# A fused S4 convolution and gated unit on one core: another split of the kernel spectrum, table casts by transfers, additions by identity matmuls, and a new static order

## The chip, the cores and the metric

The kernel runs on one core of a Trainium2 chip. The metric is the device time of one execution in microseconds (us). TensorE (PE), VectorE (DVE), ScalarE (ACT), GpSimd (POOL) and SyncE (SP) each execute their own instructions in order; SP here only issues transfers, and POOL and ACT issue some too. Work on different engines is ordered by semaphores alone. Matmuls accumulate in PSUM, from where VectorE or ScalarE has to evict a result; the other tiles lie in SBUF.

## The reference

With L = 2048 tokens, D = 512 channels, N = 128 modes per channel and F = 1792 hidden columns, all arrays in bf16:

```python
xn  = layernorm(x)                                  # over the 512 channels
dt  = exp(log_dt);  A = A_re + 1j * A_im
P   = exp(dt * A * l)                               # 512 x 128 x 2048, l is a bf16 array
K   = sum over n of (C * P * dt * B), real part     # 512 x 2048: one filter for each channel
y   = irfft(rfft(xn padded) * rfft(K padded))[:2048] + xn * Dskip
glu = (sigmoid(xn @ w_gate) * (xn @ w_up)) @ w_down
out = x + y + glu
```

The lags l are held in bf16, so above 256 they are rounded to multiples of 2, 4 and 8: only some hundreds of different lags occur, and a filter can be put together from few powers.

## The kernel before, in words

**Order.** No scheduler decides on the chip. Every piece of work is an operation of a planner (`_Plan`, `pl.add`), with an engine, dependencies and buffers to take and give back; the list `ORDER` (above line 286) then holds all operation numbers in the order in which they are emitted, and each engine runs its own in that order. Three more lists choose engines: `ON_DVE` names the evictions and copies (`pl.copy`, L287 to L290) that VectorE does, the others being ScalarE's; `UEV` names the up projections that ScalarE evicts (L1066) before VectorE's product, which for the others reads PSUM; `ON_ACT` names the row tiles whose layer norm moments ScalarE takes. PSUM has two pairs of banks (128x1024 f32) and four single banks.

**Layer norm.** 16 row tiles of 128x512. VectorE takes moments (`bn_stats` L547, `bn_aggr` L548) of 15, ScalarE (L541, L542) of one. Per group of tiles `ln_small` takes the reciprocal root, partly by `pow` on POOL (L482, L483), and VectorE a reciprocal (L508); L555 (ScalarE) or L560 (VectorE) normalises. Transposed copies of xn feed the gated unit.

**Ladder.** From dt, exp and sin (L611 to L656) VectorE makes w = exp(dt A) in f32 and squares it again and again (ScalarE squares, L672; VectorE L679 and L681): 12 levels w, w^2, w^4 ... Each level is cast to bf16 (`f_cast`), by ScalarE (L666) or VectorE (L664), into the tables `W`. The f32 levels live in three rotating buffers.

**Tables and filter.** For each of four chunks of 128 channels, complex multiplications (`cmul`: L737 and L738 multiply by the real and the imaginary part of a level, L742 and L743 add) and squares (ScalarE L790, VectorE L795 and L796) build two tables for each channel: G, 16 powers times C·dt·B, and H, 41 powers. A 32-column matmul for each channel (L821) gives all 16x41 lags. The result is evicted (`kq`), put in another order by selection matmuls (L841) and evicted as `kT`, to which VectorE adds Dskip at one row (L852). G has two buffers, used in turn by the chunks.

**Convolution.** L698 transforms xn along blocks of tokens and writes the result to DRAM (`z_scr`). 16 units follow, eight for each half of the channels: load 256 KB of `z_scr`; L892, second step of the transform, four matmuls of 64x64; eviction to `xx`; a second copy of `xx` with its 32-row halves exchanged, in the first half by four transfers of 64 KB from SBUF to SBUF, in the second by four VectorE copies (L905); load 320 KB of constants (`c_E`); L914, ten full matmuls of 256 columns, which make the filter's spectrum of that unit from `kT`; eviction to `kb`; the products L919 (2048 elements) and L923 (1024) on VectorE; L936, the first step back, 16 matmuls of 64x64; eviction; write of 256 KB to DRAM (`v_scr`). When all units of a part are written, loads of `v_scr` in another order follow, and the last step back, L995. L997 adds a correction for a few last lags, made from `f_pre` on POOL (L712 to L716), L955 and L972.

**Gated unit.** Four groups of 512 tokens; each has 14 gate projections (L1031, sigmoid L1043), 14 up projections (L1055), products (L1070) and four down projections of 14 matmuls (L1099). For the first three groups the result is evicted to `glu_sb` and x is added by accumulating transfers that POOL issues (L1136); `final` then has VectorE add that and L995's result (L1010). The last group's down projections run into the PSUM bank that L995 adds to, and VectorE adds x (L1119).

Weights and rows are loaded in an order that is written out (`load`), the gate weights in three pieces.

Of the kernel before, what the change touches and what calls it, by code (L numbers as in the profile page):

```python
# [10 lines left out]
BF = mybir.dt.bfloat16  # L11
# [8 lines left out]
L = 2048  # L20
# [11 lines left out]
NGE = 16  # L32
NH = 41
NHP = 96
CUT_G = (0, 3 * 128, 7 * 128, 14 * 128)
CUT_U = (0, 7 * 128, 14 * 128)
NU = 16
NKT = 5
# [21 lines left out]
LAG0 = [0, 1, 3, 5, 7, 6, 4, 2, 8, 10, 14, 12, 9, 11, 13, 15, 256, 262, 260, 258, 264, 266, 270, 268, 524, 520, 516, 512, 780, 776, 772, 768,  # L60
        1024, 1032, 1544, 1536, 1280, 1288, 1800, 1792, 2048]
EXP = {5: 1, 9: 1, 10: 1, 11: 3, 17: 1, 21: 1, 22: 1, 23: 3, 24: 3, 25: 1, 26: 1, 28: 3, 29: 1, 30: 1, 33: 3, 34: 3, 35: 1, 37: 3, 38: 3, 39: 1}
# [31 lines left out]
def _build_M2():  # L94
# [3 lines left out]
    for g in range(NU):  # L98
        for par in range(2):
# [17 lines left out]
            M2[g, blk, blk] = M  # L117
    return M2

def _build_MAB():  # L120
# [4 lines left out]
    for g in range(NU):  # L125
        for par in range(2):
# [27 lines left out]
            MA[g, blk, blk] = A  # L154
            MB[g, blk, blk] = B
    return MA, MB

def _row(l):

    v = int(np.float32(ml_dtypes.bfloat16(l)))  # L160
    seg = range(0, 16) if v < 256 else range(16, 24) if v < 512 else range(24, 32) if v < 1024 else range(32, 40) if v < 2048 else (40,)
    for h in seg:
        if v >= LAG0[h] and (v - LAG0[h]) % 16 == 0 and (v - LAG0[h]) // 16 < NGE:
            return h, (v - LAG0[h]) // 16
    raise ValueError(l)

def _build_E(M2, by):

    E = np.zeros((NKT, 8, NGE, NU, 128))
    z = M2.reshape(NU, 2, 2, 32, 128)  # L170
    s1 = _build_S1(64).reshape(64, NU, 2, 2)
    for l in range(L):
        h, i = _row(l)
        if h < 40:
            m = (l - 1024 * (h >= 32)) % 2048
            E[h // 8, h % 8, i] += 2.0 ** EXP.get(h, 0) * np.einsum("gpc,gpcf->gf", s1[m // 32], z[:, :, :, m % 32, :])
    E = E.reshape(NKT, 128, NU, 128).transpose(1, 2, 0, 3)[:, by]
    E[:, 1::2] = np.roll(E[:, 1::2], 64, axis=-1)
    return E

def _consts():
    S1 = _build_S1()
    M2 = _build_M2()
    MA, MB = _build_MAB()
    by = np.arange(NU).reshape(2, NU // 2).T.reshape(NU)

    def quads(m, cross=False):
        m = m.transpose(1, 0, 2)
        lo, hi = m[0:64, :, 0:64].copy(), m[64:128, :, 64:128].copy()
        if cross:  # L190
            lo[:, 1::2], hi[:, 1::2] = m[64:128, 1::2, 64:128], m[0:64, 1::2, 0:64]
        return np.concatenate([lo, hi], axis=0)

    f = lambda v: np.ascontiguousarray(v.astype(np.float32)).astype(ml_dtypes.bfloat16)
    sw = np.zeros((128, 8, 48))
    for q in range(128):
        sw[q, 2 * (q // 32) + q % 2, 16 + q % 32 // 2] = 1.0
    sr = np.zeros((128, 4, 64))
    for q in range(8):
        sr[q, q // 2, 31 + 32 * ((q ^ (q // 2)) % 2)] = 1.0  # L200
    return dict(SR=f(sr), ident=f(np.eye(128)), S1=f(np.tile(S1, (4, 1))), S2=f(np.stack([_build_S2(by), np.roll(_build_S2(by), 32, axis=1)], axis=1)), M2=f(quads(M2[by])), SW=f(sw),
                MAB=f(np.stack([quads(MA[by], True), quads(MB[by], True)], axis=2)), E=f(_build_E(M2, by).reshape(128, NU // 2, 2, NKT, 128).transpose(1, 0, 2, 3, 4)))

UEV = (3, 5, 8, 9, 10, 11, 15, 16, 17, 18, 19, 20, 21, 23, 24, 26, 27, 28, 29, 30, 31, 32, 33, 34, 35, 36, 37, 38, 39, 40, 41, 42, 43, 44, 45, 54)
ON_DVE = (64, 67, 73, 76, 97, 98, 110, 121, 122, 123, 124, 482, 836, 838)
ON_ACT = (2,)
ORDER = [
# [987 lines left out]
```

## Time and profile before

| | |
|---|---|
| runs shown | 222.72, 221.31, 222.79 us; median 222.72 |
| profiled execution | span 219.8 us from the first to the last instruction; the page gives no other time of it |
| TensorE clock granted | 0.999 |
| transfers | 41.36 MB in 40651 packets |

The median of the runs is 2.9 us above the span. The page divides the span into 40 slices and gives the busy share of each in tenths (9 is 90% or more):

```profile
PE   7999988999999999999999999999989999999994
...
DVE  3999999999999999999999999999989999993582
ACT  3699999999999999769899999977578978942000
```

TensorE and VectorE are busy almost throughout; ScalarE has room in the second half and little to do in the last eighth. In the groups, a line gives engine, operation, shapes and count, then busy time and the mean of one in ns, and then the idle time of the engine just before:

```profile
L737 DVE TENSOR_TENSOR big<-big 128x2048 bf16<-128x2048 bf16 x4 | 4.9, 1231 | 0.0
L679 DVE SCALAR_TENSOR_TENSOR big<-big 128x512 f32<-128x512 f32 x11 | 7.6, 690 | 0.0
L672 ACT ACTIVATE big<-big 128x1024 f32<-128x1024 f32 x11 | 12.4, 1129 | 0.2 <-DVE big L664 0.2
```

An instruction's busy time overlaps that of the next by a little, so in the chain of waits (the work that ended last, followed back from the end) the same instruction counts a little less.

### The profile page before, as it was taken

How to read it: one execution, taken by the hardware profiler on the slowest of the kernel's cores; microseconds unless marked ns; L12 is line 12 of the kernel's file. 1: busy time of each engine (PE TensorE's matmuls, PEld its weight loads, DVE VectorE, ACT ScalarE, POOL GpSimd, SP SyncE). 2: the span in 40 equal slices, each digit the busy share in tenths (PEclk: the TensorE clock that was granted, in tenths of full speed). 3: DMA queues.
4: the chain of work that ended last, by engine and by line, in shares of the span. 5: the costliest groups of instructions: out<-in, count | busy, mean ns of one | idle time of the engine just before them, and what ended most of it. 6: DMA issues, size and time to landing. Idle time of an engine off the chain costs nothing.

```text
span 219.8 us, 5357 instructions
## 1 busy us (share of the span) xinstructions
PE 209.2 (95%) x2075; PEld 105.0 (48%) x2103; DVE 202.2 (92%) x444; ACT 175.9 (80%) x283; POOL 22.6 (10%) x39
## 2 busy tenths in 40 slices
PE   7999988999999999999999999999989999999994
PEld 2544433444434454445555555554555455543453
DVE  3999999999999999999999999999989999993582
ACT  3699999999999999769899999977578978942000
POOL 2216001001000049100000004000020100000000
PEclk9999999999999999999999999999999999999999
DMA  5997069216667064526818579856857987688743
GB/s 172 333 425 298 7 180 317 80 42 143 237 134 206 18 198 97 202 82 178 244 55 237 152 244 210 212 173 169 228 111 236 265 265 232 189 234 209 220 158 136
DMA packets 40651, 41.36 MB, mean 188 GB/s; under 512 B 9009, under 2 KB 31922, under 8 KB 40498
## 3 DMA queue, kind: packets, MB, share of 16 engines
q1 hardware_dynamic: 39458, 39.12, 57.7%
q0 software_dynamic: 864, 1.57, 4.9%
q10 hardware_dynamic: 304, 0.33, 0.6%
q8 instruction: 16, 0.26, 0.5%
q14 instruction: 9, 0.07, 0.1%
HBM read 25.28 MB, written 12.06 MB: 170 GB/s over the span
## 4 chain that ended last, share of the span: by engine, by line
DVE 48%; PE 41%; DMA 4%; ACT 4%; issue 2%; POOL 0%; DVEq 0%; ACTq 0%
PE bank L1099 11%; DVE big L738 7%; PE pair L914 7%; DVE big L737 6%; PE bank L1031 6%; PE bank L1055 6%; DVE hT_sb L1070 6%; PE pair L936 5%; DVE stats L547 4%; DVE big L742 4%; DVE big L743 3%; DVE big L679 3%; DVE big L681 3%; DMA big<-c_E 3%; ACT big L290 3%; DVE big L613 2%
## 5 line engine op out<-in xcount | busy, mean ns | idle before, releaser
L290 ACT ACTIVATE big<-pair 128x1024 bf16<-128x1024 f32 (+2 forms) x75 | 73.4, 996 | 9.2 <-PE pair L936 1.9
L1055 PE MATMUL bank<-xnT,wu_sb 128*128 128x512 bf16 x214 | 54.4, 379 | 2.5 <-ACT us_sb L1066 1.3
L1031 PE MATMUL bank<-xnT,wg_sb 128*128 128x512 bf16 (+1 forms) x211 | 50.9, 367 | 1.4 <-ACT xnT L576 0.4
L1099 PE MATMUL bank<-wd_sb,hT_sb 128*128 128x512 bf16 (+1 forms) x230 | 50.2, 366 | 0.4
L1043 ACT ACTIVATE hT_sb<-bank 128x512 bf16<-128x512 f32 x52 | 32.1, 643 | 3.8 <-PE bank L1031 3.6
L1031 PEld LDWEIGHTS <-wg_sb 128*128 128x128 bf16 x236 | 21.9, 98 | 26.4 <-issue 5.2
L1099 PEld LDWEIGHTS <-hT_sb 128*128 128x128 bf16 x238 | 22.5, 98 | 24.8 <-issue 2.1
L1055 PEld LDWEIGHTS <-wu_sb 128*128 128x128 bf16 x224 | 21.0, 97 | 27.2 <-issue 5.4
L737 DVE TENSOR_TENSOR big<-big 128x1024 bf16<-128x1024 bf16 (+4 forms) x40 | 26.8, 670 | 0.1
L738 DVE TENSOR_TENSOR big<-big 128x1024 bf16<-128x1024 bf16 (+4 forms) x40 | 26.6, 666 | 0.0
L1066 ACT ACTIVATE us_sb<-bank 128x512 bf16<-128x512 f32 x36 | 22.4, 634 | 0.0
L919 DVE TENSOR_TENSOR big<-big 128x2048 bf16<-128x2048 bf16 x16 | 19.5, 1219 | 0.4
L914 PE MATMUL pair<-big 128*128 128x256 bf16 x160 | 19.8, 272 | 0.1
L914 PEld LDWEIGHTS <-big 128*128 128x128 bf16 x160 | 15.5, 98 | 4.9 <-issue 1.1
L790 ACT ACTIVATE sq_sb<-big 128x256 bf16<-128x256 bf16 (+2 forms) x20 | 13.7, 685 | 3.9 <-DVE big L743 3.8
L743 DVE TENSOR_TENSOR big<-big 128x512 bf16<-128x512 bf16 (+4 forms) x40 | 16.6, 414 | 0.0
L742 DVE TENSOR_TENSOR big<-big 128x512 bf16<-128x512 bf16 (+4 forms) x40 | 16.5, 413 | 0.0
L290 ACT ACTIVATE big<-big 128x256 bf16<-128x256 bf16 x36 | 15.7, 470 | 0.2
L1070 DVE TENSOR_TENSOR hT_sb<-hT_sb,us_sb 128x512 bf16<-128x512 bf16 x36 | 14.9, 421 | 0.0
L905 DVE COPY big<-big 32x1024 bf16<-32x1024 bf16 x32 | 13.5, 421 | 0.5
L1070 DVE TENSOR_TENSOR hT_sb<-hT_sb,bank 128x512 bf16<-128x512 bf16 x20 | 13.2, 684 | 0.5 <-PE bank L1055 0.5
L936 PE MATMUL pair<-big 64*64 64x512 bf16 (+1 forms) x256 | 12.8, 326 | 0.5 <-ACT big L290 0.2
(103 smaller groups left out, 222.2 us busy)
## 6 DMA issues: line engine op xcount, KB each, us to landing
big<-c_E SPq DMA_DIRECT2D x16, 320.0 KB, 4.4
z_scr<-big SPq DMA_DIRECT2D x16, 256.0 KB, 3.0
big<-z_scr SPq DMA_DIRECT2D x16, 256.0 KB, 3.5
v_scr<-big SPq DMA_DIRECT2D x16, 256.0 KB, 2.9
big<-in_A_u_dram SPq DMA_DIRECT2D x4, 512.0 KB, 8.5
big<-big SPq DMA_DIRECT2D x32, 64.0 KB, 3.1
big<-v_scr SPq DMA_DIRECT2D x4, 512.0 KB, 5.0
wu_sb<-in_B_w_up_dram SPq DMA_DIRECT2D x2, 896.0 KB
```

The lines of the kernel that those rows point to most:

```text
L290: nc.scalar.activation(out=get(out), in_=get(in_), func=ACT.Identity)
L737: V.tensor_tensor(out=wide(outp), in0=wide(lo), in1=mre, op=ALU.mult)
L738: V.tensor_tensor(out=wide(tb()), in0=wide(lo), in1=mim, op=ALU.mult)
L742: V.tensor_tensor(out=outp[:, :, 0], in0=outp[:, :, 0], in1=tb()[:, :, 1], op=opr)
L743: V.tensor_tensor(out=outp[:, :, 1], in0=outp[:, :, 1], in1=tb()[:, :, 0], op=opi)
L914: T.matmul(two(sk)[:, o:o + DW], es()[:, g, kt, :], kT[p][:, kt, :], start=kt in (0, NKT - 1), stop=kt >= NKT - 2)
L936: T.matmul(two(sv)[o:o + 64, DW * (2 * g + y):2 * DW * (g + 1)], mab[b:b + 64, 2 * u + g, q, :], pq()[b:b + 64, q, ch] if y else pp()[b:b ...
L1031: T.matmul(bank(sl, k % 2)[:, c0:c1], w_at(w, CUT_G, kt, k), xnT[:, grp, kt, c0:c1], start=(kt == 0), stop=(kt == KT - 1))
L1043: S.activation(out=hT_sb[:, hs.idx, k % 2, :], in_=bank(sl), func=ACT.Sigmoid)
L1055: T.matmul(bank(sl), w_at(wu_sb, CUT_U, kt, k), xnT[:, grp, kt, :], start=(kt == 0), stop=(kt == KT - 1))
L1070: V.tensor_tensor(out=h(), in0=h(), in1=us_sb[:, us.idx, :] if on else bank(sl), op=ALU.mult)
L1099: T.matmul(bank(po)[:, 0:c[1] - c[0]], hT_sb[:, hts[k // 2].idx, k % 2, jj * 128:(jj + 1) * 128], wd_sb[:, k, c[0]:c[1]], start=first and ...
```

## The change

- **Tables.** G now has 32 entries for each channel, H 21. H is made for two chunks at once. G has one buffer instead of two. L821's matmul (now L847) is 64 rows by 42 columns.
- **Spectrum in two steps.** The selection matmuls, `kT` and `c_E` go. After both chunks of a half, `f_y` (L878) multiplies `kq` by a small constant (`Y1`); the result (`ys`) is evicted and written to DRAM (`y_scr`, 1.7 MB for each half). Each unit loads two pieces of 104 KB of it, and `fk` (L955) makes the unit's spectrum with 16 matmuls of 52 rows and 32 columns each from a second constant (`Y2`) that stays in SBUF. Dskip enters through a table `dz` in the first step. The correction of the last lags (L955, L972, L997, `f_pre`, `f_rz`) goes.
- **Swap.** The rows are in another order, so that the second copy of `xx` exchanges neighbouring rows; one `stream_shuffle` on VectorE for each unit (L936) does it, on 512 32-bit elements, in both halves. The matmuls of the steps L892 and L936 (now L927 and L980) are 32 columns wide, and twice as many.
- **Ladder.** Ten squarings instead of eleven. Each of the 11 levels is cast by a transfer that POOL issues (L717, f32 in SBUF to bf16 in SBUF). The square has a buffer of its own.
- **Moments.** ScalarE takes those of seven row tiles instead of one; POOL has two more small operations in each group of four tiles that has such tiles (L524, L525).
- **Last additions.** The residual is put into PSUM by a matmul with an identity (L1018 for `glu_sb`, L1115 for x in the last group), L1024 and L1010 add to it there, and VectorE or ScalarE evicts plainly (`pl.copy`, L327 and L329). `final` works on four row tiles and one half of the channels.
- **Order.** `ORDER`, `ON_DVE` (24 numbers instead of 14), `UEV`, the buffer addresses and the order of the loads are new; the gate weights come in four pieces, the first one smaller.

The diff, cut to its core:

```diff
-ON_ACT = (2,)
+ON_ACT = (2, 6, 7, 10, 11, 14, 15)
...
+            on = [i for i in range(t0, t1) if i in ON_ACT]
+            if on:
+                r = slice(on[0], on[-1] + 1)
+                P.tensor_tensor(out=mq[:, r], in0=mvs[:, r, 0], in1=mvs[:, r, 0], op=ALU.mult)
+                P.tensor_tensor(out=mvb[:, r, 1], in0=mvs[:, r, 1], in1=mq[:, r], op=ALU.subtract)
             P.tensor_scalar(out=q["ve_b"], in0=mvb[:, s, 1], scalar1=EPS, scalar2=None, op0=ALU.add)
             P.tensor_tensor(out=q["sd_b"], in0=q["ve_b"], in1=half[:, s], op=ALU.pow)
...
-                V.tensor_copy(out=W[p][:, k], in_=cur[:, :, DW * p:DW * p + DW])
...
-                S.activation(out=W[p][:, k], in_=cur[:, :, DW * p:DW * p + DW], func=ACT.Identity)
...
+        def f_cw(cur=cur, k=k):
+            with nc.allow_non_contiguous_dma(reason="laid out"):
+                P.dma_start(out=W_all[:, :, k], in_=cur)
...
-        G = at(OFF["G"] + 8 * KB * (c % 2), [NPR, 2, NGE, 2])
+        G = at(OFF["G"], [NPR, 2, NGE, 2])
...
+                        for t in range(4):
+                            b = 32 * t
...
+                            i_ = dz[b:b + 32, p:p + 1, :] if kind == "d" else kq[b:b + 32, 2 * hs_.start + rr:2 * (hs_.stop - 1) + rr + 1:2 * hs_.step, :]
+                            T.matmul(pb[:, cs_, :], y1[b:b + 32, w, :], i_, start=first, stop=True, tile_position=(b, 0), skip_group_check=True)
...
+            ys_st[p].append(dma("SP", y_scr[p][:, hr, :], ys[p][:, hr, :], deps=y_evs[n], prio=PC, pkt=8192 if n == 0 else 5120, rel=[])
...
-                def f_sw(xx=xx):
-                    for b in range(4):
-                        V.tensor_copy(out=half_of(xx, b, 1), in_=half_of(xx, b ^ 1, 0))
...
+            def f_sw(xx=xx):
+                q = lambda j: xx()[:, j].rearrange("p h m -> p (h m)").bitcast(I32)
+                V.stream_shuffle(out=q(1), in_=q(0), mask=[i ^ 1 for i in range(32)])
...
-                for g in range(2):
-                    for kt in range(NKT):
-                        o = DW * g + (2 * DW if kt == NKT - 1 else 0)
-                        T.matmul(two(sk)[:, o:o + DW], es()[:, g, kt, :], kT[p][:, kt, :], start=kt in (0, NKT - 1), stop=kt >= NKT - 2)
...
+                for kk in range(2):
+                    for x in range(2):
+                        for j in range(2):
+                            for g in range(2):
+                                o, b = 64 * x + 32 * j, 64 * g
+                                T.matmul(two(sk)[o:o + 32, 2 * DW * g + DW * kk:2 * DW * g + DW * kk + DW], y2[b:b + 2 * NHH, u, 2 * x + j, kk, :],
+                                         es()[b:b + 2 * NHH, x ^ g, j, :], start=True, stop=True, tile_position=(b, o))
...
+        def fr():
+            for h in range(2):
+                T.matmul(bank(sl, h), ident[:], res[:, 2 * h:2 * h + 2, :], start=True, stop=False, skip_group_check=True)
...
-            V.tensor_tensor(out=ot().rearrange("p r d -> p (r d)"), in0=two(sl), in1=res.rearrange("p r d -> p (r d)"), op=ALU.add)
...
+        fin = pl.copy(nc, 0.90, lambda: res, lambda: two(sl).rearrange("p (q d) -> p q d", q=4), [my], 30, rel=[sl])
...
+                if res:
+                    T.matmul(bank(po)[:, 0:c[1] - c[0]], ident[:], res()[:, jj, c[0]:c[1]], start=first, stop=False, skip_group_check=True)
...
-                        V.tensor_tensor(out=ot()[:, r, c0:c1], in0=bank(po)[:, 0:c1 - c0], in1=xt[:, jj, c0:c1], op=ALU.add)
```

By engine the new order has these instructions (before, after): TensorE 4208 and 5040 with weight loads, VectorE 408 and 328, ScalarE 269 and 247, POOL 40 and 36, SP 98 and 101. VectorE's L556 takes the reciprocal of the group's standard deviations, as L508 did; POOL's order around the ladder is six casts, the four operations L524 to L527 of one group, three casts, the four of the next group, and two casts.

More of the change, by code (lines that the diff above doesn't have):

```diff
@@ L153, in _build_MAB @@
                 B[32 + 16:64, 32:64] = -2 * np.sin(t64)[16:32]
-            MA[g, blk, blk] = A
-            MB[g, blk, blk] = B
+            MA[g, blk, blk][_perm(s)] = A
+            MB[g, blk, blk][_perm(s)] = B
     return MA, MB
[L158 to L179, printed above, removed]
+def _perm(s):
+    k = np.arange(32)
+    h, r = (k % 2, k // 2) if s else (k // 16, k % 16)
+    return np.concatenate([32 * h + 2 * r, 32 * h + 2 * r + 1])
@@ L279, in add, with copy @@
         return op
-    def copy(self, nc, cost, out, in_, *args, **kw):
+    def copy(self, nc, cost, out, in_, *args, scale=None, **kw):
         get = lambda v: v() if callable(v) else v
@@ L286, in fcopy @@
         def fcopy():
-            if dve:
+            if not dve:
+                nc.scalar.activation(out=get(out), in_=get(in_), func=ACT.Identity, scale=1.0 if scale is None else scale)
+            elif scale is None:
                 nc.vector.tensor_copy(out=get(out), in_=get(in_))
             else:
-                nc.scalar.activation(out=get(out), in_=get(in_), func=ACT.Identity)
+                nc.vector.tensor_scalar(out=get(out), in0=get(in_), scalar1=scale, scalar2=None, op0=ALU.mult)
         return self.add("DVE" if dve else "ACT", cost, fcopy, *args, **kw)
@@ L412 @@
     VPART = ((0, 0, NU // 2), (1, 0, NU // 2 - 2), (1, NU // 2 - 2, NU // 2))
+    y_scr = [dram.tile([128, NHH, DW], BF, name="y_scr%d" % p) for p in range(NP)]
     v_scr = [dram.tile([4 * (u1 - u0), 128, DW], BF, name="v_scr%d" % n) for n, (p, u0, u1) in enumerate(VPART)]
@@ L451 @@
     l_wg, l_wu = [], []
-    piece = lambda k: 0 if k < 3 else 1 if k < 7 else 2
+    piece = lambda k, cut=CUT_G: max(n for n in range(len(cut) - 1) if cut[n] <= 128 * k)
     def w_at(w, cut, kt, k):
@@ L457, in w_at @@
         return w[:, o:o + 128]
-    for n in range(3):
+    for n in range(4):
         fs_ = slice(KT * CUT_G[n], KT * CUT_G[n + 1])
@@ L502, in fm_ @@
         def fm_():
-            S.activation(out=q["m_f"], in_=mvb[:, s, 0], func=ACT.Identity)
-        o_s = pl.add("POOL", 1.4, fn, deps, prio)
+            a_ = [i for i in range(t0, t1) if i not in ON_ACT]
+            b_ = [i for i in range(t0, t1) if i in ON_ACT]
+            S.activation(out=lnt["m_f"][:, a_[0]:a_[-1] + 1], in_=mvb[:, a_[0]:a_[-1] + 1, 0], func=ACT.Identity)
+            if b_:
+                S.activation(out=lnt["m_f"][:, b_[0]:b_[-1] + 1], in_=mvs[:, b_[0]:b_[-1] + 1, 0], func=ACT.Identity)
+        o_s = pl.add("POOL", 2.6, fn, deps, prio)
         sm_ = pl.add("ACT", 0.2, fm_, deps, prio)
@@ L811 @@
+        tdeps = g_done + [hm] + list(h_ops.values())
         evs, mm = [], None
@@ L1136, in facc @@
                         P.dma_start(out=fx(), in_=xv[:, i - 1:i + 1, :], accum_op=ALU.add)
-                acc = [pl.add("POOL", 1.0, facc, ges[-2:], PGE, dma=(256 * KB, _rate(1024), 1.0))]
-                final(i // 2, acc)
+                acc = acc[:jj // 2] + [pl.add("POOL", 1.0, facc, ges[-2:], PGE, dma=(256 * KB, _rate(1024), 1.0))]
+        if grp not in LATE:
+            for p in range(NP):
+                final(grp, p, acc)
     order = list(pl.run())
```

505 lines of the change are left out of this document (262 added, 243 removed), and 77 rows, old and new, of the table ORDER.

## The prediction

> **What bounds the kernel now.** I read the page's busy times first, then the windows of three stages, then the chain of waits, then the groups by form and the transfers. The windows (start:end, length; then busy us of PE, weight loads, DVE, ACT, POOL; clock; DMA share; GB/s):
>
> ```profile
> PE 209.2 (95%) x2075; PEld 105.0 (48%) x2103; DVE 202.2 (92%) x444; ACT 175.9 (80%) x283; POOL 22.6 (10%) x39
> ...
> 0.00:107.00 107.00, 102.04 (x886) 46.69 (x899) 102.22 (x251) 98.13 (x169) 18.16 (x32) 1.00 0.57 178
> 107.00:194.00 87.00, 84.84 (x1036) 47.05 (x1052) 85.29 (x171) 74.65 (x111) 4.48 (x7) 1.00 0.72 200
> 194.00:220.00 26.00, 22.30 (x163) 11.24 (x157) 14.65 (x25) 3.12 (x4) 0.00 (x0) 0.99 0.63 189
> ```
>
> The reader is to see that VectorE and TensorE are both full until 194, that ScalarE has 21 us free there, and that afterwards only TensorE is. 194 is where the last product of the convolution (L923) ends. Up to it VectorE's own view counts 6.1 us idle, 3.4 of them the wait for the first input; so 187.9 us of it are work and 2.7 are holes.
>
> The chain of waits (start, length, engine, line), at the shares and at the end:
>
> ```profile
> DVE 48%; PE 41%; DMA 4%; ACT 4%; issue 2%; POOL 0%; DVEq 0%; ACTq 0%
> ...
> 70.51 1.14 DVE big L737
> ...
> 193.58 1.42 PE pair L936 x32
> ...
> 199.26 3.13 PE bank L1099 x14
> 202.39 0.98 PE pair L995 x8
> ...
> 213.33 3.18 PE bank L1099 x28
> 216.53 0.42 DVE big L1119
> ```
>
> To about 107 it runs over VectorE, afterwards mostly over TensorE. From the last product's end to the end of the span 25.8 us pass: L936 ends at 195.0, its result goes to DRAM and back, the first L995 that needs it runs at 202.4, TensorE ends at 216.5, and eviction and last output take 3.3. I also take the prices from the chain's pieces, since an instruction's mean in a group overlaps the next by some 0.085 us: 2048 bf16 products 1.14 against a mean of 1.22.
>
> **VectorE up to the last product.** Prices, by form:
>
> ```profile
> L905 DVE COPY big<-big 32x1024 bf16<-32x1024 bf16 x32 | 13.5, 421 | 0.5
> L664 DVE CAST big<-big 128x512 bf16<-128x512 f32 x8 | 3.1, 427 | 0.0
> L681 DVE TENSOR_TENSOR big<-big 128x512 f32<-128x512 f32 x11 | 7.6, 691 | 0.0
> L914 PE MATMUL pair<-big 128*128 128x256 bf16 x160 | 19.8, 272 | 0.1
> ```
>
> Gone: 32 swap copies L905 x 0.43 = 13.7; 8 casts L664 x 0.34 = 2.7; the ladder's 11th step, two of 0.60 = 1.2; the Dskip additions 0.8; 6 of 15 moment passes (L547 and L548, 0.80) = 4.8; 4 of 11 normalisations (L560) x 0.33 = 1.3. Sum 24.5.
> Added: 16 shuffles (L936 of the new file) of 512 32-bit elements. No row shows one. The bounds are 0.335 (a bf16 instruction over 512) and 0.69 (the whole mean of L681); I take 0.60, what an f32 instruction over 512 costs on the chain, as the same count and width: 9.6. Evictions and copies handed to VectorE before the last product, 11.9 us at 0.60 (512) and 1.14 (1024) against 2.3 before: 9.6. Tables: the first (G) doubles to 32 entries, 35.3 to 66 us, the second (H) halves to 21 with fewer steps; by instructions and sizes 81.1 becomes 81.9, among it 3.1 for strided forms whose runs are two elements (0.29 for 256 elements where plain ones fall to 0.2). GLU products that the order moves ahead of the last product: 4.3. Small ones 0.3. Sum +24.6. So +0.1, about nothing: VectorE's work before the last product doesn't shrink, only its kind changes.
>
> **TensorE.** The kernel spectrum took 160 full matmuls, ten in 1.09 on the chain, 17.5 in all. It becomes 16 per unit on 64 by 32 tiles, four side by side; priced like L892's four in 0.3 plus 0.1 for the change of tile form, 0.41 each, 6.6 in all: -10.9. Selection matmuls L841 go: -3.5. The first step (L878) adds 8 sets of 0.55 to 0.7: +5.0. Products on wider columns +0.3. Identity matmuls for x and for the GLU result, 0.216 a piece, +3.5; the rank corrections and their transposes go, -1.1; forms changed more often, about -1 to 0. Sum -8, to 201. ScalarE: casts -9.8, a ladder square, squares and evictions given away, against six moment pairs of 1.45 (+8.7): -11.
>
> **New waits.** First, the ladder casts. VectorE and ScalarE wrote the bf16 tables; now POOL issues an 11 x 512 KB converting transfer. VectorE's order leaves, between the ladder step and the first product that reads the cast, 3.3 us for level 4 (three products with a bank, one without, one ladder step), 5.7 for level 6 and 4.2 for level 7; buffers come round with over 7. The nearest rows:
>
> ```profile
> DMA to landing us min/median/max: 4.7/5.3/6.8
> ...
> big<-big SPq DMA_DIRECT2D x32, 64.0 KB, 3.1
> ```
>
> The first are POOL's own accumulating transfers (L1136, 256 KB, 0.86 to 1.19 to issue), the second SBUF to SBUF on SP's queue. At 3.1 nothing waits; at 5.3 levels 4 and 7 wait 2.1 and 1.1; at 6.8 the waits are 3.6, 1.2 and 2.7, 7.5 in all. The cast shares its queue with one row and its memory with the other, so I take the middle, 4.2: 1.0 us of wait. Behind it stand all table products, as VectorE issues in order. The Trainium skill (DMA: Bandwidth & Descriptors, "Anatomy of one DMA — SWDGE (gpsimd) path") fits 2.0 us plus bytes over 436 GB/s; for 512 KB that is an estimate of 3.2, no wait at all and 216.9 in place of my forecast, but for L1136's 256 KB it gives 2.6 where this trace has 5.3, so here I hold the rows above it.
>
> Second, POOL's moments. In after, VectorE takes the reciprocal (L556) only when POOL has done four small operations (L524 to L527, two of them new), which stand behind cast 5 on POOL. VectorE has 3.7 us of other work after that cast's ladder step, less 1.0 for POOL's issue: a cover of 2.7. The old pair took 0.46 and 1.23; two more at 0.22 to 0.45 make 2.1 to 2.6. I price it at 0; the cover is thin, and it is the last rival below.
>
> Third, the spectrum goes through DRAM. Write and load take 3.0 and 3.5 by the rows of z_scr, with evictions about 10; in the order 14 us of VectorE work (second half; 33 in the first) lie between. Hidden; without that cover it would cost up to 10, once. The queue of SP gets two loads of 104 KB per unit for one of 320 KB (4.4), and loses the 32 swap issues, so it isn't later. The table buffers become single: between chunks 1.6 to 3 us of products cover 2 us of matmuls; 0, at most 1 each.
>
> **The tail.** The order now has every GLU product and eviction of the last group ahead. After the last L980 (1.0 after the product) TensorE has 0.43 of identity matmuls, two down projections with residual (0.22 + 3.02 each) and 0.43 again, 7.4, beside a round trip that I put at 8 (7.4 before, from 195.0 to 202.4, plus 0.6 for the load that may have been hidden). Then 7.4 of matmuls remain (two halves of the last projection 3.3, the inverse step and the rest 4.1), and 3.3 to the end: 1.0 + 8.0 + 7.4 + 3.3 = 19.7, with 0.2 for form changes 19.9. That is 5.9 less than 25.8: before, 14.1 us lie between L995's start at 202.4 and TensorE's end at 216.5, now 7.4, since two projections of 3.2 run earlier, beside the round trip.
>
> **The sum.** 3.4 + 187.9 + 2.7 + 0.1 + 1.0 + 19.9 = 215.0 against the span of 219.8. The median of the runs shown, 222.72, is 2.9 above the span (the lowest, 221.31, 1.5), and so I predict 215.0 + 2.9 = 217.9. TensorE alone would allow 219.8 - 8 = 211.8.
>
> **Rivals.**
> A, as above: VectorE stays the bound, the gain is the tail's. With landings from 3.1 to 5.3 it is 216.9 to 220.1.
> B: shuffles as cheap as 0.335 (-4.2) and no cast wait. VectorE would give 209.8, TensorE's 211.8 then binds: 214.7. For it: an engine that only moves data in bf16 is that fast (L664). Against: the shuffle sees 32-bit elements. Its lowest corner is VectorE's 209.8 + 2.9 = 212.7.
> C: the casts land like L1136's worst, 6.8, since they carry twice its bytes in 256-row strips: waits 7.5, span 221.5, 224.4: no difference that can be measured. Against it: no DRAM side.
> D, slower: POOL's moments starve while VectorE streams. In the trace one 128x4 operation on POOL took long beside back-to-back products:
>
> ```profile
> L714 POOL TENSOR_TENSOR pre<-pre,xnT x3: 224/445/5439, 81.2 to 82.1; 128x4 f32<-128x4 f32 x3
> ```
>
> If both new ones take 5.44, the group lasts 10.9 + 1.7 = 12.6, VectorE waits 9.9 at L556 and the time is 227.8. It decides from a group of 9.8 us. Against it: the old group's reciprocal shows no idle time, and L1136 issued in 0.86 to 1.19 with VectorE full. The Trainium skill (SBUF — State Buffer, "Who interferes with whom") has such a rule, an exclusive lock on a port pair shared by VectorE and GpSimd that also holds up the writing of descriptors; L714's 5.44 us agrees, L1136's issue times don't show it.
>
> **Chances.** A 0.46, B 0.26, C 0.15, D 0.13. Within 1% (220.5 to 225.0) is about what a measurement of this kernel can tell from no change. Faster: B and nearly all of A, 0.70. Same: C and A's edge, 0.16. Slower: D and a hair of C, 0.14. The range runs from B's corner, 212.7, to C's 224.4, and leaves out D: 212.5 to 224.5.
>
> **What would show it.** VectorE's last product should end near 195, not 190 (B) or over 200 (C, D); shuffles near 0.6 to 0.69 in the groups; casts landing in 3 to 5.3, with VectorE idle before L773 at most 3; POOL's L524 and L525 under 0.5 each; TensorE's busy time near 201; 20 us after the last product. I am wrong if VectorE has holes of over 3 us ahead of the products, most likely from the DRAM round trip or the single table buffers, or if the tail is again 25.

## The result and the profile after

The changed kernel takes 233.3 us (median of four, 231.0 to 234.2) against 222.8 for the one before in the same session: a ratio of 1.048, interval 1.043 to 1.053. It is slower, outside the range, where 217.9 was predicted. The profiled execution is the lowest of the four, with a span of 228.3, which the sum of the prediction put at 215.0. All times of single waits and instructions below are of one profiled execution each.

The page of the changed kernel: busy times, three rows of tenths (work of PE, its granted clock, work of DVE) and the transfers.

```profile
PE 207.7 (91%) x2486; PEld 98.4 (43%) x2519; DVE 196.9 (86%) x359; ACT 172.1 (75%) x264; POOL 26.8 (12%) x43
...
PE   7899896799999899999999899999998998899694
...
DVE  4999693999999999999999999998898999882242
...
PEclk9999999799999999999999999999999999999979
...
DMA packets 50187, 44.61 MB, mean 195 GB/s; under 512 B 9072, under 2 KB 44400, under 8 KB 49776
```

VectorE has 5.3 us less to do than before and TensorE 1.5, and yet the span is 8.5 longer. There is a hole near 40 us in the rows of PE and DVE, the granted clock falls there and once more at the end, and the transfers carry 3.25 MB more. The windows of the changed kernel (start:end, length; PE, weight loads, DVE, ACT, POOL; clock; DMA share; GB/s):

```profile
0.00:107.00 107.00, 98.67 (x733) 45.73 (x744) 95.99 (x196) 89.30 (x153) 24.91 (x41) 0.98 0.68 180
107.00:205.00 98.00, 91.31 (x1620) 43.01 (x1646) 94.49 (x157) 80.78 (x109) 1.90 (x3) 1.00 0.75 212
205.00:228.00 23.00, 17.75 (x143) 9.66 (x129) 6.42 (x7) 2.01 (x3) 0.00 (x0) 0.93 0.74 199
```

The last product of the convolution (L966) ends at 204.9; before it was 194, forecast was 195. What VectorE waits for in the changed kernel (in total, times, longest):

```profile
DVE big L721 <- DMA big<-big: 5.6, 2, 3.8
DVE stats L594 <- DMA big<-in_A_u_dram: 3.2, 1, 3.2
...
DVE big L329 <- PE pair L980: 2.4, 3, 0.9
DVE big L329 <- PE pair L878: 0.8, 1, 0.8
```

L721 is a ladder step. It doesn't read a cast; it overwrites the f32 buffer that a cast transfer still reads. POOL's timeline shows when the casts were issued (start, length, line, and in brackets how long POOL had idled before and what released it), the next line how long the casts took to land, and VectorE's timeline which steps stood:

```profile
17.45 0.92 POOL L717 DMA_DIRECT2D big<-big  x1 [8.83 <-DVE big L686]
20.20 0.75 POOL L717 DMA_DIRECT2D big<-big  x1 [1.83 <-DVE big L723]
23.40 0.72 POOL L717 DMA_DIRECT2D big<-big  x1 [2.44 <-DVE big L723]
31.14 0.72 POOL L717 DMA_DIRECT2D big<-big  x1 [7.03 <-DVE big L723]
35.29 1.43 POOL L717 DMA_DIRECT2D big<-big  x2 [3.43 <-DVE big L774]
```
```profile
DMA to landing us min/median/max: 3.1/4.2/8.9
```
```profile
26.36 0.69 DVE L721 SCALAR_TENSOR_TENSOR big<-big 128x512 f32<-128x512 f32 x1 [1.85 <-DMA big<-big]
39.09 0.69 DVE L721 SCALAR_TENSOR_TENSOR big<-big 128x512 f32<-128x512 f32 x1 [3.77 <-DMA big<-big]
```

Two different things are seen. The first cast was issued at 17.45 and its buffer came free only at 26.3, 8.9 us later, while the weights were being loaded. And the fourth issue, at 31.14, is level 4: in `ORDER` the cast of level 3 (operation 65) stands behind that of level 4 (68) and behind the first table product. It goes out with level 5 at 35.29, released by a table product (L774) though it doesn't read what that makes, and its own source was ready at 27.65. The step that needs its buffer waits 3.77 us.

The end in the chain of waits of the changed kernel (start, length, what):

```profile
204.93 0.82 PE pair L980 x32
...
205.77 1.24 DVE big L329
...
207.03 3.90 DMA v_scr<-big
...
210.99 4.83 DMA big<-v_scr
...
215.87 0.85 PE bank L1010 x4
...
222.85 1.53 PE bank L1118 x14
```

The round trip lasts from 205.75 to 215.87, 10.1 us where 8.0 was forecast; TensorE runs out of other work 2.2 us before it ends and restarts at half the clock. In the groups by form (busy, mean ns, idle before) the priced terms stand, first of the changed kernel, then one of the kernel before:

```profile
L936 DVE STREAM_SHUFFLE big<-big 128x512 int32<-128x512 int32 x16 | 11.4, 731 | 0.0
...
L847 PE MATMUL pair<-big 128*64 128x42 bf16 x512 | 9.1, 187 | 1.4 <-DVE hT_sb L1086 0.8 <-DVE big L824 0.5
...
L955 PE MATMUL pair<-big 52*32 52x256 bf16 x256 | 6.6, 273 | 0.3
...
L525 POOL TENSOR_TENSOR mvb<-mvs,mq 128x2 bf16<-128x2 f32 x3 | 1.6, 534 | 0.6 <-ACT glu_sb L589 0.5
L524 POOL TENSOR_TENSOR mq<-mvs 128x2 f32<-128x2 f32 x3 | 1.4, 466 | 27.0 <-ACT glu_sb L588 27.0
...
L556 DVE RECIPROCAL ln_ri_f<-ln_sd_b 128x4 f32<-128x4 bf16 x3 | 0.5, 168 | 0.0
```
```profile
L821 PE MATMUL pair<-big 128*32 128x82 bf16 x512 | 6.0, 201 | 0.1
```

### The profile page after: what moved, and what is told of

The parts are those of the page before. It is cut to its first block, busy times and chain, and to the rows that moved or that the text cites. A ratio compares the mean times of both kernels' runs of the same rounds, so it can differ in the third digit from the quotient of the medians.

```text
span 228.3 us, 6087 instructions
## 1 busy us (share of the span) xinstructions
PE 207.7 (91%) x2486; PEld 98.4 (43%) x2519; DVE 196.9 (86%) x359; ACT 172.1 (75%) x264; POOL 26.8 (12%) x43
## 5 line engine op out<-in xcount | busy, mean ns | idle before, releaser
L327 ACT ACTIVATE big<-pair 128x1024 bf16<-128x1024 f32 (+2 forms) x78 | 74.5, 994 | 16.5 <-PE pair L927 4.2
L1071 PE MATMUL bank<-xnT,wu_sb 128*128 128x512 bf16 x211 | 53.0, 379 | 3.0 <-DVE hT_sb L1086 1.6
L1059 ACT ACTIVATE hT_sb<-bank 128x512 bf16<-128x512 f32 x52 | 30.0, 623 | 0.4 <-PE bank L1047 0.3
L773 DVE TENSOR_TENSOR big<-big 128x2048 bf16<-128x2048 bf16 (+4 forms) x34 | 28.8, 846 | 0.7 <-DMA big<-big 0.2
L774 DVE TENSOR_TENSOR big<-big 128x2048 bf16<-128x2048 bf16 (+4 forms) x34 | 28.5, 838 | 0.0
L962 DVE TENSOR_TENSOR big<-big 128x2048 bf16<-128x2048 bf16 x16 | 19.5, 1218 | 0.3
L778 DVE TENSOR_TENSOR big<-big 128x1024 bf16<-128x1024 bf16 (+4 forms) x34 | 16.8, 494 | 0.2
L779 DVE TENSOR_TENSOR big<-big 128x1024 bf16<-128x1024 bf16 (+4 forms) x34 | 16.7, 491 | 0.0
L327 ACT ACTIVATE big<-bank 128x512 bf16<-128x512 f32 (+1 forms) x4 | 2.2, 541 | 18.5 <-PE bank L1010 12.9
L329 DVE CAST big<-pair 128x1024 bf16<-128x1024 f32 (+2 forms) x12 | 13.1, 1093 | 3.3 <-PE pair L980 2.4
L712 ACT ACTIVATE big<-big 128x1024 f32<-128x1024 f32 x10 | 10.6, 1056 | 6.5 <-DVE big L723 6.4
L980 PE MATMUL pair<-big 64*32 64x256 bf16 (+1 forms) x512 | 13.3, 324 | 1.5 <-ACT big L327 1.2
L717 POOL DMA_DIRECT2D big<-big x11 | 8.3, 752 | 33.6 <-DVE big L723 21.4
L721 DVE SCALAR_TENSOR_TENSOR big<-big 128x512 f32<-128x512 f32 x10 | 6.8, 685 | 5.6 <-DMA big<-big 5.6
```

The costliest lines, as they stand in the source:

```text
L327: nc.scalar.activation(out=get(out), in_=get(in_), func=ACT.Identity, scale=1.0 if scale is None else scale)
L773: V.tensor_tensor(out=wide(outp), in0=wide(lo), in1=mre, op=ALU.mult)
L774: V.tensor_tensor(out=wide(tb()), in0=wide(lo), in1=mim, op=ALU.mult)
L778: V.tensor_tensor(out=outp[:, :, 0], in0=outp[:, :, 0], in1=tb()[:, :, 1], op=opr)
L779: V.tensor_tensor(out=outp[:, :, 1], in0=outp[:, :, 1], in1=tb()[:, :, 0], op=opi)
L962: V.tensor_tensor(out=pp().rearrange("p q h m -> p (q h) m"), in0=xx().rearrange("p q h m -> p (q h) m"), in1=kb()[:, 0:2 * DW].unsqueeze( ...
```

## The experiments

All are edits of the changed kernel; the numbers in `ORDER` and `ON_DVE` are operations. Ratios are to the kernel before, with the interval. All but e2 and e4 have e1's edit of `ORDER`. In e1, e2 and e3 that list is wrapped in fewer lines, so their line numbers are lower by 8 (L713 is L721 of the changed kernel, L765 L773).

**Is it the casts?** The cast of level 3 in its place (e1); the down weights loaded later (e2); the casts by ScalarE (e3).

```diff
# e1
-... 578, 579, 63, 555, ... 563, 565, 567, 574, 167, 566, 65, 70, ...
+... 578, 579, 63, 65, 555, ... 563, 565, 567, 574, 167, 566, 70, ...
# e2: without e1's edit; operation 18 moved from behind 74 to behind 62
-l_wd = load("SP", wd_sb[:], B_w_down, 1792 * KB, pkt=14336)
+l_wd = load("ACT", wd_sb[:], B_w_down, 1792 * KB, pkt=14336)
# e3: with e1's edit
-                P.dma_start(out=W_all[:, :, k], in_=cur)
-        c_op = pl.add("POOL", 1.0, f_cw, ...)
+            S.activation(out=W_all[:, :, k], in_=cur, func=ACT.Identity)
+        c_op = pl.add("ACT", 0.95, f_cw, ...)
```

> One number moved in the written order: the cast of ladder level 3 is issued right after its level is made, ahead of that of level 4, instead of after the first table product. Theory V (VectorE's in-order chain is the bound up to the last product, so each of its waits costs its length): the wait of 3.8 us at the sixth ladder step goes, with TensorE's idle 3.0 us behind it and the 3.4 us of half clock that follow; the last product ends 3.5 to 4 us earlier, the span is near 224.5, the time 229 to 230, ratio to before about 1.03. Rival P (TensorE or a transfer is the bound later on and absorbs the wait): the wait goes but the time stays within 1 us, 232 to 234.

Measured: 227.8 us, 1.026 [1.022, 1.029], 5.5 less than the changed kernel and more than theory V gave. In its profile the last product ends at 201.4, 3.5 earlier, and neither stretch at half clock is left. VectorE's waits for casts in e1:

```profile
DVE big L713 <- DMA big<-big: 1.1, 2, 0.7
...
DVE big L765 <- DMA big<-big: 0.7, 1, 0.7
```

> The 1.8 MB load of the down projection's weights is issued by ScalarE at about 23 us instead of by SyncE at 11.4 us; nothing else. Theory V with the loads as the cause of the first wait: cast 0 lands in 3 to 5 us instead of 8.9, the wait of 1.85 us at the third ladder step goes, the time falls by 1.5 to 2 us to about 231.5, the second wait of 3.8 stays. Rival Q (the cast is late because POOL is late in writing its descriptors while VectorE is busy): cast 0 still lands after over 8 us and the time stays at 233.

Measured: 234.1, 1.053 [1.050, 1.056], no gain. The casts now land in 3.1 to 5.0 us (before that edit 3.1 to 8.9), so the weights were what held the first one. But the misplaced cast is still there, and now both a ladder step and the first product wait, in e2:

```profile
DVE big L713 <- DMA big<-big: 3.8, 1, 3.8
...
DVE big L765 <- DMA big<-big: 2.2, 2, 2.0
```

> The eleven casts are done by ScalarE, one instruction of 1024 elements each, at about 0.95 us (level 3 in its turn as in the first run); no cast transfer is left. Theory V: both waits of VectorE go, ScalarE has 10.5 us more work but also lost 5 us of waits in that stretch; the time falls by 4 to 6 us, to 227 to 229. Rival P: no change, or slower by the delay of ScalarE's sigmoids, 233 or more.

Measured: 237.8, 1.070 [1.067, 1.072], 10 us worse than e1. VectorE now waits for ScalarE, in e3:

```profile
DVE big L764 <- ACT big L708: 3.5, 1, 3.5
DVE hT_sb L1077 <- ACT us_sb L1073: 3.1, 3, 1.5
```

So casts by ScalarE alone cost more than the transfers do in this order (the old split between ScalarE and VectorE was not run); and one cast in the wrong place costs about 5 us of the 11.

**Is VectorE the bound, and where?** Copies in place of the shuffles in the changed kernel (e4) and in e1 (e7); nine evictions of the second half from VectorE to ScalarE (e6); moments of all but one row tile back on VectorE (e8).

```diff
# e4, e7
-                V.stream_shuffle(out=q(1), in_=q(0), mask=[i ^ 1 for i in range(32)])
+                V.tensor_copy(out=xx()[:, 1], in_=xx()[:, 0])
# e6
-ON_DVE = (..., 235, 289, 291, 295, 297, 300, 331, 361, 413, 422, 474, 610, ...)
+ON_DVE = (..., 235, 289, 610, ...)
# e8
-ON_ACT = (2, 6, 7, 10, 11, 14, 15)
+ON_ACT = (2,)
```

> The 16 shuffles are replaced by plain bf16 copies of the same data (the exchange of rows is left out). Theory V: 0.65 becomes about 0.33 each, VectorE has 5 us less to do ahead of the last product, the time falls by 4 to 5 us, to 228.5 to 229.5. Rival P (TensorE is the bound in the second half): under 1 us.

Measured: 232.1, 1.045 [1.039, 1.050]: 1.2 less than the changed kernel, with intervals that overlap, and not the 4 to 5 of theory V.

> On top of the early cast of level 3 (227.8 us): plain bf16 copies in the place of the 16 shuffles (the exchange of rows is left out), as in the earlier run but without its disturbances of TensorE's clock. Theory V: VectorE 5 us less, time 222.5 to 224. Rival P: 226.5 to 228.

Measured: 228.9, 1.030 [1.024, 1.036]. On the page VectorE has 4.2 us less work than in e1, and nothing is gained. In the profile the last product ends 1.0 us earlier, at 200.3, and the tail loses that again: TensorE idles 3.2 us there and the clock is 0.57 from 212 to 216.

> On top of the early cast of level 3 (227.8 us): nine PSUM evictions of the convolution (four of the first spectrum step, five of 1024 columns) go from VectorE back to ScalarE, which has 16 us idle between 130 and 205. Theory V (VectorE bounds up to the last product): 8 us less of VectorE's work and 2.4 us less of its waits, time 4 to 6 us lower, 222 to 224. Rival P (the stage is set by the chain from unit to unit over all engines, with TensorE): under 1.5 us of gain, or a loss where ScalarE's queue delays sigmoids.

Measured: 232.8, 1.048 [1.044, 1.052], 5 us worse than e1: VectorE waits for ScalarE's evictions in front of its shuffles (6.1) and products (4.2). ScalarE has no room there in this order: it is busy for 29.6 of the 31 us from 154 to 185.

> On top of the early cast of level 3 (227.8 us): VectorE takes the moments of six more row tiles again (as before the change), ScalarE six pairs less, POOL's two added operations for each group go. Theory V: VectorE's work in the first 100 us grows by 4.8 us and the time with it, to 231 to 233. Rival P (VectorE has slack there): 227 to 229.

Measured: 232.3, 1.045 [1.039, 1.051]: 4.5 us worse than e1 for 4.4 us more of VectorE's work on the page, all of it in the first half. There VectorE binds one for one; in the second half it doesn't.

**Why is the tail long?** Half of one down projection moved ahead into the round trip (e5); the loads of `v_scr` that are ready put ahead of the last write (f1); only the two small ones ahead of one large (g1); g1 with e5's edit (g2); f1 with more (f2, f3); and the last loads reading rows that were written earlier (p3).

```diff
# e5: operation 874 behind 700; the first half of the last group's last projection without L1010 ahead of it
-... 870, 700, 525, 526, ... 699, 864, 611, 874, 701, ...
+... 870, 700, 874, 525, 526, ... 699, 864, 611, 701, ...
# f1
-... 608, 519, 866, 475, 870, 700, 525, 526, 520, 609, 610, 516, 517, 523, 522, ...
+... 608, 519, 525, 516, 522, 866, 475, 870, 700, 526, 520, 609, 610, 517, 523, ...
# g1
-... 609, 610, 516, 517, 523, 522, ...
+... 609, 610, 517, 523, 516, 522, ...
# f2: f1, e5, the cast of level 2 (62) right behind its step; f3: f1, that cast, e2's load
# p3
-            v_v = v_scr[n][:].rearrange(...)
+            v_v = (v_scr[1][0:8] if n == 2 else v_scr[n][:]).rearrange(...)
```

> On top of the early cast of level 3 (227.8 us): of the last projection of 256 columns the first half (1.64 us of TensorE) is issued ahead of the inverse steps that wait for the last load of v_scr, and its inverse step comes behind it. Theory T (the tail waits for the round trip of v_scr, 3.05 us of TensorE idle there): the idle falls to about 1.4 and the time by 1.6 us, to 226.2. Rival L (the tail is set by what follows the last load, evictions and output transfers): the wait shrinks but the time stays within 0.6.

Measured: 228.0, 1.025 [1.018, 1.032], as e1. TensorE's waits for the loads of `v_scr` fall from 3.3 to 2.45 us in total, and the round trip gets longer, from 10.5 to 11.1.

> On top of the early cast of level 3 (227.8 us): three loads of 384 KB of the earlier part of v_scr are issued by SyncE ahead of the write of the last unit instead of behind it; no arithmetic changes. Theory B (the last loads are slow since 1.2 MB stand in the transfer engines at the same time; without the wait for the last write 3.3 us were gained): the last small loads land in about 3 us instead of 4.8 or more, TensorE's wait ahead of the last inverse step falls from 3 to about 1, time 225.5 to 226. Theory T (only the write and load of the last unit themselves count): the wait stays at 2.5 to 3, time 227.5 to 228.

Measured: 231.5, 1.041 [1.034, 1.048], 3.7 worse than e1. The chain of f1 says why: the last write, which took 3.5 us in e1, is now issued behind the loads and takes 7.4. TensorE then waits 5.5 us for the loads that need it, and the clock is 0.57 from 212 to 220.

```profile
204.24 7.43 DMA v_scr<-big
```

> On top of the early cast of level 3 (227.8 us), the opposite of the last trial: of the five loads that SyncE issues behind the last unit's write, one of 384 KB moves behind the two small ones, which wait for that write, so that less stands in the transfer engines while the write and the small loads run. Theory B (the write and the loads share the transfer engines and run in the order of issue): the write lands in about 3 us, ScalarE's two loads in 3 to 4 instead of 5, TensorE's wait of 3 us falls to 1 or 1.5, time 226 to 226.5. Theory T: no change, 227.5 to 228.

Measured: 226.9, 1.020 [1.016, 1.023], between the two theories and 0.9 below e1, with intervals that just touch. The write of g1 is quick again (3.2 us), and the large load behind the small ones is slow:

```profile
209.03 7.46 DMA big<-v_scr
```

> The same with half of the last projection ahead of the inverse step that waits. Under theory B what is left of the wait is covered: 225 to 226. If the late large loads become the wait in their turn: as the one before or slower.

Measured: 225.6, 1.016 [1.009, 1.023]; by the median the best version with all the work, and still slower than the kernel before. Its interval overlaps that of g1.

> The loads moved as above, the casts in the order of their levels (levels 2 and 3 right behind their ladder steps), and half of the last projection ahead of the inverse step that waits. If theory B holds and the end is TensorE's: 224 to 225.5. If output transfers bind the end: no better than the moved loads alone.

Measured: 230.8, 1.037 [1.030, 1.044].

> The loads moved, the casts in the order of their levels, and the down projection's weights loaded from ScalarE's queue behind the third cast. When only the weights were moved, the first wait went and came back 2 us later at the first product. With the casts in order nothing is left for it to come back to: the remaining waits of VectorE on casts (0.7, 0.4 and 0.7 us) go, and the time falls by 1 to 1.5 us below the moved loads alone; if contention among transfers only moves again, by less than 0.5.

Measured: 231.7, 1.041 [1.031, 1.050]. Neither f2 nor f3 makes up for f1's edit; in f3 a cast still takes up to 7.5 us to land.

> On top of the early cast of level 3 (227.8 us): the loads that wait for the last two units' part of v_scr read a part that was written earlier (so the last two units' values are wrong), at the same place of the queues and of the same size. Theory T (the tail waits for the write and load of the last unit): TensorE's idle 3.05 us goes, 2.5 to 3 us less, 225 or so. Rival B (the loads are slow because the transfer engines are full at the end, not because they wait for the write): under 1 us.

Measured: 224.5, 1.011 [1.007, 1.015], 3.3 less than e1 and near theory T's 225. The last loads needn't wait for the last write any more, and still end at 213.6, against 214.0 in e1, but TensorE has only 0.8 us of waiting for them in place of 3.3. Its clock is 0.998 to 1.000 in all four runs; in e1's it was 0.990 to 0.992 in three and 1.000 in one.

**What binds the second half?** Half of the matmuls of L980 left out (p2); that and copies for the shuffles (p4); then also half of the columns of two evictions of each unit (q1); q1 with p3's edit (q2).

```diff
# p2, p4, q1, q2
-                for n in range(4):
+                for n in (0, 2):
# q1, q2: the eviction of L955, likewise that of L980, in the second half's units
-... kb().rearrange("p (k g d) -> p g k d", k=2, g=2)
+... kb().rearrange("p (k g d) -> p g k d", k=2, g=2)[:, 0:2 - p]
```

> On top of the early cast of level 3 (227.8 us): half of the inverse step's matmuls (L980, 12.3 us of TensorE in all) are left out, so that 6 us less of TensorE's work lie in the second half; nothing else changes. Theory P (behind the tables TensorE bounds): 3.5 to 6 us less, 222 to 224. Theory C (behind the tables the units run through TensorE, an eviction, VectorE, TensorE and an eviction in a fixed order, so that no single engine's work sets the time): under 2.5 us, 225.5 to 227.5, as when VectorE had 5 us less.

Measured: 228.4, 1.027 [1.024, 1.029]. TensorE loses 3.8 us of work on the page, and nothing is gained.

> On top of the early cast of level 3 (227.8 us): both at once, plain copies for the shuffles (VectorE 5 us less) and half of the inverse step's matmuls (TensorE 6 us less); both parts of the computation are left out. Theory C (both engines are full behind the tables): more than the two alone together, 4 to 6 us less, 222 to 224. Theory P: the same as with half of the inverse step alone.

Measured: 227.6, 1.023 [1.019, 1.026]. On the page VectorE loses 4.3 us and TensorE 3.1; the gain is 0.2. Where most of it went is in what TensorE waits for in p4, between 145 and 200 us: ScalarE's evictions, for which it waits 1.0 us in e1 in front of the same three lines.

```profile
PE pair L980 <- ACT big L327: 1.8, 4, 0.5
PE pair L955 <- ACT big L327: 1.2, 3, 0.5
PE pair L927 <- ACT big L327: 1.1, 1, 1.1
```

> Leaves out half of the columns of two evictions in each unit of the second half (the spectrum's and the first step back's), beside a copy in place of each shuffle and half of the matmuls of the first step back, with the cast of level 3 in its place. VectorE has some 5 us less work, TensorE 3, and now ScalarE some 5 and VectorE 2 more less. Theory S: the second half is bound by the three engines together, so that what VectorE and TensorE save is lost to waits for ScalarE's evictions (4.8 us on TensorE and 3.4 on VectorE in the kernel without this cut); then the last product starts at 196 or earlier, against 199.4, and the time falls to 223.5 to 225. Theory R: the transfers set the second half; then the last product stays at 198.5 to 199.5 and the time at 227 to 228.

Measured: 227.0, 1.021 [1.017, 1.024], the time that R gave; the last product (L962) of the profiled execution starts at 200.6, with the clock at 0.89 from 175 to 190, so later than either had it.

> The same, and the last loads of the second half's result read rows that were written earlier, so that they needn't wait for the last write (wrong rows). Theory S: both gains add, 220 to 222. Theory R: no less than the 224.5 that the loads alone gave. If the loads then stand in each other's way at the end, the product comes earlier as in the other kernel but the time is 223 to 224.5.

Measured: 223.2, 1.005 [1.003, 1.008]; the last product starts at 197.8, where p3 has it at 199.3. The time lies between the two theories. From e1 to q2 the page's busy times fall by 5.6 us on TensorE, 5.5 on VectorE and 6.5 on ScalarE, and beside p3's gain 1.4 to 1.6 us come of it. ScalarE now waits for the write that should free the buffer it evicts into (4.0 us, against 0.3 in e1); first q2's waits of ScalarE from 145 to 200, then the transfers on q2's chain:

```profile
ACT big L327 <- DMA v_scr<-big: 4.0, 4, 1.4
```
```profile
171.11 4.34 DMA v_scr<-big
...
184.92 5.34 DMA v_scr<-big
...
190.98 4.01 DMA v_scr<-big
...
195.72 3.28 DMA v_scr<-big
...
199.07 5.34 DMA big<-v_scr
```

In the kernel before such a write of 256 KB took 2.9 us in the median; a chain picks out slow ones, so the comparison is rough. The window from 190 to 200, first of the kernel before, then of q2; the last two columns are DMA share and GB/s:

```profile
190.00:200.00 10.00, 9.89 (x84) 4.92 (x84) 8.89 (x21) 4.99 (x7) 0.00 (x0) 1.00 0.82 221
```
```profile
190.00:200.00 10.00, 8.11 (x119) 3.57 (x119) 8.68 (x12) 5.41 (x8) 0.00 (x0) 1.00 0.97 268
```

In the profiles the last product (L966) ends at 201.4 in e1, 200.3 in e7, 203.0 in p2, 200.0 in p4 and 199.6 in q2, against 194.0 in the kernel before: the cuts bring it forward by 1.8 us at most.

So in the second half of e1 TensorE and VectorE are nearly full (28.3 and 28.1 of the 30 us from 160 to 190), ScalarE too in that stretch (28.1) though not around it, and the transfers are at 0.79 to 0.96 of their time from 160 to 200. Taking work from one or two engines shows the next; with work taken from all three, waits for transfers appear. That the transfers then set the time is read from q2's chain and not tested: no run made the transfers lighter, and none changed the fixed order in which the units pass through the engines, which p2's theory C names and which stays a rival.

## Why the prediction was wrong, point by point

The profiled execution against the forecast's path over VectorE (215.0 to 228.3):

| term | forecast | measured | difference |
|---|---|---|---|
| first wait | 3.4 | 3.2 | -0.2 |
| VectorE's work to the last product | 188.0 | 190.5 | +2.5 |
| waits for casts | 1.0 | 5.8 | +4.8 |
| other holes | 2.7 | 5.5 | +2.8 |
| from the last product to the end | 19.9 | 23.4 | +3.5 |

That is the span. From the span to the time it is 2.7 where I had 2.9, and the median of 233.3 is 2.3 above this execution, the lowest of four.

- **The casts: the step that failed.** "Buffers come round with over 7" was worked out as if the casts went out in the order of the levels. They don't: level 3 goes behind level 4 and a table product, and then its buffer is wanted at once. The median landing was right (4.2, the value I took), but the first cast took 8.9, outside my bounds of 3.1 to 6.8, as the nearest rows were of stages without the weight loads; that is past the 7 us of cover and made the wait of 1.85. Moving one number in the list brought 5.5 us (e1): 4.0 of these waits are gone, and in its profile both stretches at half clock.
- **Other holes.** I carried over the 2.7 of the kernel before and put nothing on waits ahead of the evictions that VectorE takes over. They came to 2.3 us up to the last product (L329 for L878 and L980), and 0.6 ahead of a shuffle; the kernel before has one such wait, of 0.7 (L852).
- **VectorE's work.** The shuffles cost 0.65 each net of the overlap, where I took 0.60 (+0.8 in all), and tables and squares came out 2.1 higher than before, where I had 0.8. Small misses with the sign against me. That VectorE's work there doesn't shrink was right.
- **TensorE.** I had -8, where my own terms add up to -6.7 to -7.7. Over the lines of the convolution and of the last additions it fell by 4.2, start to start, from the kernel before to e1. The busy times of the page don't show that: 209.2 before, 207.7 after and 209.5 in e1, but e1's trace has a record of every matmul (2519, as many as weight loads), while 28 are missing before and 33 after. The spectrum (L955) at 6.6 and the first step at 5.0 were right within 1. The mis-sized term is the lag matmul: 512 of 128x42 take 8.9 us start to start against 5.9 for 512 of 128x82, though each moves half the columns; I had +0.3 for all products on wider columns.
- **The tail.** Moving two projections ahead did shorten it, from 25.8 to 23.4, but the round trip took 10.1, not 8.0, so TensorE idled 2.2 us and then lost about 1.7 at half clock. I took the trip's length from the kernel before and didn't ask what else its transfers would share the engines with. f1 and g1 show them in each other's way: whichever is put first makes the other late. p3, where the last loads needn't wait for the write, takes 3.3 off the time of e1.
- **Rivals.** D didn't occur: the two new operations of POOL take 0.47 and 0.53 in the mean and L556 shows no idle time. C had the right place, a late cast, by another mechanism and at 7.5 against 5.8. B's cheap shuffle is refuted (0.65, not 0.335), and p2 shows that TensorE alone wasn't next. Slower had a chance of 0.14, nearly all of it for D's mechanism, so no mechanism of the forecast gives the time that was measured.
- **What no step of mine had.** I added up VectorE and TensorE, and took ScalarE and the transfers as room. ScalarE was to lose 11 us of work and lost 3.8 (175.9 to 172.1). Its room in the second half is an average: e6 shows that nine evictions more cost 5 us, and q2 that the transfers are close behind. What stays open is the rest: g2, with the casts in place and a better tail, is 1.6% above the kernel before, some 3.6 us. In its profile the tail behind the last product is 3.4 us shorter than before (22.4 against 25.8), and that product ends 7.6 later (201.6 against 194.0), so the loss lies ahead of it. VectorE's 2.5 us of work, its waits for casts (2.0 in g2) and ahead of evictions, the transfers' 3.25 MB and the lag matmuls' 3.0 would each be part of it; I didn't try them apart. The gain of p3 also has two parts that I didn't part, the shorter wait and the kept clock.

## What to carry to other kernels

When an order is written out by hand, read the emitted order of every operation that frees a rotating buffer; the dependencies alone don't say when a buffer comes back. Here a cast that was emitted behind a table product went out only when that product was done, though it reads nothing of it; that its destination, which is strided over the whole of `W`, overlaps what the product reads is the likely reason, but no run tested it. Price a transfer by rows from the same stage, since its landing is set by what is in flight beside it. And where three engines are near full and the transfers too, a cut on one of them was worth nothing here; name who is next first: a run that leaves work out tells that quickly.

## What the runs showed of the hardware

- In the changed kernel the granted clock fell to half after TensorE had idled 3.0 us (to 41.1) and 2.2 us (to 215.9): 0.72 from 40 to 44 and 0.85 from 44 to 48, which makes 3.4 us at half, and 0.50 from 216 to 219. After 4.7 us of idle time in e2 it was 0.51 from 40 to 44 and 0.64 from 44 to 48, which makes 6.8. In e4 1.8 us of idle time was enough (0.58 from 198 to 202); in e1 one of 3.0 near 213 had no such sequel. The Trainium skill (TensorE: Matmul & The Clock Gate, "Part 1: The HAM clock gate") describes a free-running window of about 3.4 us and half rate after an idle one; lengths and irregularity agree, though the idle times in the changed kernel and in e4 were shorter than such a window.
- A converting transfer of a level lands in 3.1 us at best and 8.9 at worst, and the last write of 256 KB in 3.5 (e1) and 7.4 (f1), with the same bytes in the same pattern; what was in flight beside them differed.
- A shuffle of 512 32-bit elements costs a little more than an f32 instruction of that width: 731 ns in the mean against 685 (L721), or 0.65 us net of the overlap against 0.60.
- The columns alone didn't price these narrow matmuls: 512 of 128x42 into 64 rows took 8.9 us start to start, half as much again as 512 of 128x82 into 32 rows (5.9).
